# VectorE's first tap product in the PSUM words that TensorE sums; 2816 rows held back; a new order

## The chip, the cores and the metric

One core of one Trainium2 chip runs the program. The metric is device time in microseconds (us). Engines are written as the profile has them: PE is TensorE's matmuls and PEld its weight loads, DVE is VectorE, ACT is ScalarE, POOL is GpSimd, SP is SyncE, which issues most DMAs.

## The reference

A windowed mix of 7 tokens with softmax weights per head, then a top-1 mixture of experts over its result.

```python
# attention: B=8, S=3584, D=192, H=8 heads, K=7 taps, group=24
w = softmax(weight_gen, axis=-1)                      # [B, S, 8, 7]
out = einsum('bshk,bskhg->bshg', w, x_unf)            # x_unf[s, k] = x[s - 6 + k], zeros before 0
# experts: N=28672 tokens, D=192, E=8, F=1024
e_idx = argmax(x @ w_gate, axis=1)
for e in range(E):
    h = maximum(x[mask] @ w1[e], 0.0)                 # mask: e_idx == e
    out[mask] = gate_w[mask, None] * eom[mask, e, None] * (h @ w2[e])
```

`gate_w` is the softmax probability of the chosen expert, `eom` the sigmoid of `x @ w_output_gate`.

## The kernel before

**Units.** The 28672 tokens are cut into 32 units of 896 (128 partitions by 7 tokens). For each unit the front end loads x and the weights (SyncE), makes the softmax (VectorE, ScalarE), forms seven tap products of 128x1344 (x shifted by a tap, times that tap's weight), adds them, splits the sum into fp16 high and low parts in one of three row buffers `rt` (`sum_steps`), computes gate logits, ranks the tokens within their experts (`rank`: VectorE's scan, then two small TensorE matmuls `ps<-p,upper` and `ps<-p,ones`), and GpSimd scatters the rows into `srtd` in DRAM, sorted by expert: seven indirect DMAs for each unit.

**Taps.** `TAPS` gives a unit's first taps to GpSimd (`gap` tiles in SBUF) and the rest to VectorE. For units 0 to 5 (`u < PE_U`) GpSimd makes 4 and VectorE 3 (`vap` tiles in SBUF), and TensorE adds all seven by fp32 matmuls with an identity (`cf`) into one of two places of 1536 words in PSUM (`sum_free`, at 0 and 2560): per tap three matmuls, of 512, 512 and 320 columns (`add_steps`). A place comes free when VectorE has split the sum. From unit 6 on VectorE adds alone, into an accumulator in PSUM (`acc_steps`); there GpSimd makes 5 or 4 taps, by `POOL` and `SHARES`.

**Weights.** During the first units the weights of the 8 experts are loaded, split into fp16 pairs and written to `wd` in DRAM (`weight_steps`, `split_steps`).

**Tiles.** After each unit, `plan_rounds` decides how many expert tiles of a size may be released: rows that have come so far, less the rows taken, less a number that is held back (`HOLD`, six times the tile's rows: 3072 for 512). A released tile belongs to an expert that has enough rows; a slot that finds none points at dummy rows. `tile_load` has SyncE load the tile's rows transposed (`xT`), and the expert's weights (`wa`, `wb`, or `late` near the end), and TensorE does five matmuls for each of 8 blocks of hidden columns (`ps<-xT,wa`), ScalarE and VectorE make `hh` and `hl` from them, and TensorE 24 matmuls for each 128 rows (`ps<-wb,hh` and `ps<-wb,hl`). GpSimd scatters the results. There are 5 tiles of 256 rows after unit 2, 7 of 384 after units 4 to 6, then 43 of 512, and 5 of 256 and 15 of 128 among the last.

**Order.** Nothing is scheduled on the chip: every engine runs its instructions in the order in which this code writes them. `Order` is a planner that keeps a clock for each engine, and at each step lets the chain of work go on that can start first; among equals the rank decides (`RANK_...`), and `FAVOUR` moves single chains. Its costs are the constants at the end of the file (`LAT_P`, `LANDED`, `LAT_R` from VectorE's scan to the ranking matmul, and so on). So a changed constant moves instructions on all engines.

**Stirring.** `stir` puts matmuls on zeros (`ps<-pad,ident`, 256 columns) into TensorE's queue where the planner sees a gap over `STIR[0]` us, half as long as the gap; into an open sum, or, with a start flag, into a free place.

Of the kernel before, what the change touches and what calls it, by code (L numbers as in the profile page):

```python
# [27 lines left out]
def plan_rounds(units, every, size):  # L28

    left, rounds = 0, {}  # L30
    for u in range(units):
        left += size
        last = u == units - 1
        if u not in every and not last:
            continue
        subs = []
        for T, keep in SIZES(u, last):
            n = max(0, -(-(left - keep - HOLD(T)) // T))
            while n > 0:
                k = min(n, 8)  # L40
                subs.append((T, k))
                left -= k * T
                n -= k
        if last:
            subs.append((128, (left + NE * TAILK) // 128))
        rounds[u] = subs
    return rounds
# [259 lines left out]
def kernel(ctx: ExitStack, tc: tile.TileContext, x, wg, wgate, wogate, w1, w2, cst, out):  # L307
# [194 lines left out]
    def stir(gap):  # L502

        words, new = state["open"], False
        free = [at for t, at in sum_free if t <= T_.t]
        if words is None and free:
            words, new = ps[:, free[0] : free[0] + 256], True
        if gap < STIR[0] or words is None:
            return
        for _ in range(int(STIR[1] * gap / 0.112)):  # L510
            nc.tensor.matmul(words[:, 0:256], lhsT=ident, rhs=pad[:, 0:128].bitcast(F16), start=new, stop=new, skip_group_check=True)
# [139 lines left out]
    def load_steps():  # L651
        for u in range(1, NU):
            od.named(f"load {u}")
            od.cur.rank = (RANK_X if u <= X_EARLY else RANK_A, -1)
            yield from take(w_free, SP)
            w_load(u)
            U[u]["wt"] = od.cur.t
            od.cur.t = od.now
            od.add(softmax_steps(u), (RANK_A, u, 0), V, U[u]["wt"])
            yield from take(x_free, SP)  # L660
            if u >= XN:
                yield SP, lambda: "zero" in U[u - XN + 1]
            x_load(u)
            U[u]["xt"] = od.cur.t
            od.cur.t = od.now
# [43 lines left out]
    def tap_steps(eng, tag):  # L709

        for u in range(NU):
# [9 lines left out]
            if u >= PE_U and tag == "va":  # L721
                yield from acc_steps(u, taps)
                continue
            pairs = PAIRS if u < PE_U and tag == "ga" else 0
# [18 lines left out]
            used(u, tag)  # L743

# [50 lines left out]
    def add_steps(u, t, tag, kind):  # L795

        d = U[u]
        yield T_, lambda: "sum" in d or ("begun" not in d and (u == 0 or "sum" in U[u - 1]))
        if "begun" not in d:
            d["begun"] = 0  # L800
            _, at = yield from take(sum_free, T_)
            d["sum"], d["sum_at"] = ps[:, at : at + 1536], at
        n, flat = d["begun"], t.rearrange("p a b -> p (a b)")
        d["begun"] += 1
        for lo in (0, 512, 1024):
            hi = min(lo + 512, NV * GD)
            T_.matmul(d["sum"][:, lo:hi], lhsT=cf[:, 0:128], rhs=flat[:, lo:hi], start=(n == 0), stop=(n == K - 1 - PAIRS), skip_group_check=True)
# [3 lines left out]
        if n == K - 1 - PAIRS and state["open"] is d["sum"]:  # L811
            state["open"] = None
        if n == K - 1 - PAIRS:
# [305 lines left out]
    def tile_steps():  # L1119

        while "all" not in state or queue:
# [14 lines left out]
            d["ready"] = od.cur.t  # L1136
# [250 lines left out]
HOLD = lambda T: 6 * T  # L1387
TAILK = 79
RANK_W = 4.5
LAT = 0.0756  # L1390
LAT_S = 0.2324
LAT_P = 0.3614
LAT_T = 1.8143
LOCK = True
ARRIVE = 1.9478
LANDED = 0.5447
LAT_R = 1.1028
SLACK = 0.0352
SCATTER = 0.987
SMALL = 0.0762  # L1400
EAGER = 0, 0.2, (2, 3, 4)
BACK = 1.0
TURNS = (1536,)
# [15 lines left out]
POOL = (5,5,4)  # L1419
SHARES = {18: 5, 11: 4, 28: 4, 20: 4}  # L1420
FAVOUR = {}
PE_U = 6
STIR = 0.8, 0.5
GIVE = 1
RANK_X = 2.5
X_EARLY = 3
RANK_GATE = 4.5
FIRST_G = ()
DEFER = 4
WBX = 3.3548  # L1430
# [4 lines left out]
EARLY = {2: ((256, 0),), 4: ((384, 0),), 5: ((384, 0),), 6: ((384, 0),)}  # L1435
# [20 lines left out]
```

## Time and profile before

| | us |
|---|---|
| median of 3 runs (lowest, highest) | 1220.73 (1212.9, 1223.78) |
| profiled execution: its own time | 1223.71 |
| profiled execution: span | 1222.0 |
| PE busy in the span | 1120.0 |
| DVE busy | 955.9 |
| POOL busy | 841.5 |
| ACT busy | 616.6 |
| mean granted TensorE clock | 0.978 |

The span runs from the first to the last instruction of one execution. Busy time of an engine leaves out the time in which it waits. A stretch of the span has to be looked at by itself, since the first 150 us are spent on the front end and the weights, the middle on both the front end and the tiles, and the last 200 us on tiles alone. [...]

### The profile page before, as it was taken

How to read it: one execution, taken by the hardware profiler on the slowest of the kernel's cores; microseconds unless marked ns; L12 is line 12 of the kernel's file. 1: busy time of each engine (PE TensorE's matmuls, PEld its weight loads, DVE VectorE, ACT ScalarE, POOL GpSimd, SP SyncE). 2: the span in 40 equal slices, each digit the busy share in tenths (PEclk: the TensorE clock that was granted, in tenths of full speed). 3: DMA queues.
4: the chain of work that ended last, by engine and by line, in shares of the span. 5: the costliest groups of instructions: out<-in, count | busy, mean ns of one | idle time of the engine just before them, and what ended most of it. 6: DMA issues, size and time to landing. Idle time of an engine off the chain costs nothing.

```text
span 1222.0 us, 27128 instructions
## 1 busy us (share of the span) xinstructions
PE 1120.0 (92%) x9693; PEld 812.1 (66%) x9693; DVE 955.9 (78%) x1874; ACT 616.6 (50%) x1300; POOL 841.5 (69%) x620
## 2 busy tenths in 40 slices
PE   8987686899979999999999998899999999999897
PEld 4544375677657666666666666676666666798697
DVE  7999696999999979998999989899998653333231
ACT  4986553455555545455555544455544434434342
POOL 6678783777898868887888877678888554322122
PEclk9999898999989999999999999899999999999999
DMA  8989699998697979799799969887979696599992
GB/s 280 285 276 299 194 287 268 215 270 235 172 264 176 260 225 232 164 250 233 192 244 249 253 163 246 235 212 197 236 193 195 192 270 196 165 292 244 321 292 84
DMA packets 294952, 282.77 MB, mean 231 GB/s; under 512 B 229222, under 2 KB 254423, under 8 KB 294816
## 3 DMA queue, kind: packets, MB, share of 16 engines
q1 hardware_dynamic: 272976, 236.54, 73.0%
q0 software_dynamic: 21696, 44.30, 12.5%
q8 instruction: 76, 1.25, 0.4%
q14 instruction: 60, 0.49, 0.1%
q10 hardware_dynamic: 144, 0.20, 0.1%
HBM read 174.77 MB, written 60.28 MB: 192 GB/s over the span
## 4 chain that ended last, share of the span: by engine, by line
PE 58%; DVE 17%; DMA 9%; issue 8%; POOL 5%; ACT 1%; SPq 1%; another core or an unknown queue 0%; POOLq 0%; DVEq 0%; ACTq 0%
PE ps L207 58%; DVE ps L207 9%; DVE hl L207 4%; DMA wa<-wd 4%; POOL srtd L207 3%; DMA srtd<-rt,posi 2%; POOL gap L207 1%; DVE vt L207 1%; SPq L175 1%; DMA gt<-rt 1%; DMA meta<-srtd 1%; DVE rt L207 1%; POOL out_dram L207 1%; DVE lz L207 1%; DMA w<-in_wg_dram 1%
## 5 line engine op out<-in xcount | busy, mean ns | idle before, releaser
L207 PE MATMUL ps<-xT,wa 128*128 128x512 f16 (+3 forms) x2440 | 491.1, 350 | 42.5 <-DMA wa<-wd 12.8
L207 PE MATMUL ps<-wb,hh 128*128 128x192 f16 x3648 | 473.5, 247 | 8.2 <-ACT ys L207 4.4
L207 PE MATMUL ps<-wb,hl 128*128 128x192 f16 x1824 | 450.1, 247 | 1.4 <-issue 1.4
L207 DVE SCALAR_TENSOR_TENSOR hl<-ps,hh 128x512 f16<-128x512 f32 (+1 forms) x470 | 305.2, 666 | 172.0 <-ACT hh L207 124.0
L207 POOL TENSOR_TENSOR gap<-x,w 128x1344 f32<-128x1344 f32 x145 | 379.4, 2624 | 43.2 <-issue 14.8
L207 POOL DMA_INDIRECT out_dram<-ys,meta x220 | 218.4, 993 | 243.2 <-ACT ys L207 176.1
L207 PEld LDWEIGHTS <-wa 128*128 128x128 f16 x2440 | 226.8, 99 | 229.0 <-issue 47.7
L207 PEld LDWEIGHTS <-hh 128*128 128x128 f16 x3648 | 332.5, 98 | 53.7 <-issue 15.9
L207 ACT ACTIVATE hh<-ps 128x512 f16<-128x512 f32 (+1 forms) x470 | 267.7, 582 | 177.6 <-PE ps L207 147.9
L207 POOL DMA_INDIRECT srtd<-rt,posi x224 | 230.2, 1028 | 85.2 <-issue 57.8
L207 ACT ACTIVATE ys<-ps,sc 128x192 f32<-128x192 f32 x228 | 95.8, 420 | 288.4 <-PE ps L207 180.1
L207 DVE TENSOR_TENSOR ps<-ps,gap 128x1344 f32<-128x1344 f32 x121 | 187.9, 1553 | 0.4
L207 PEld LDWEIGHTS <-hl 128*128 128x128 f16 x1824 | 179.3, 98 | 0.9 <-issue 0.6
L207 DVE SCALAR_TENSOR_TENSOR rt<-ps,sx,rt 128x448 f16<-128x448 f32 x64 | 57.6, 910 | 7.4 <-DMA srtd<-rt,posi 2.5
L207 PE MATMUL ps<-xT,late 128*128 128x128 f16 (+2 forms) x560 | 59.9, 263 | 3.7 <-DMA late<-wd 3.7
L207 PE MATMUL ps<-gap,cf 128*128 128x512 f32 x144 | 60.7, 559 | 0.0
L207 DVE TENSOR_TENSOR ps<-ps,vt 128x1344 f32<-128x1344 f32 x35 | 54.4, 1555 | 0.0
L207 DVE TENSOR_TENSOR vt<-x,ps 128x1344 f32<-128x1344 f32 x35 | 54.1, 1545 | 0.1
L207 PEld LDWEIGHTS <-late 128*128 128x128 f16 x560 | 40.2, 98 | 16.5 <-DMA late<-wd 3.9
L207 ACT ACTIVATE rt<-ps 128x1344 bf16<-128x1344 f32 x32 | 41.3, 1291 | 17.2 <-DVE ps L207 9.5
L207 ACT ACTIVATE rt<-ps,sx 128x1344 f16<-128x1344 f32 x32 | 44.2, 1380 | 11.4 <-DVE sx L207 8.2
L207 PE MATMUL ps<-gm,gt 128*128 128x32 f16 x672 | 28.1, 177 | 20.1 <-ACT gt L207 10.4
(121 smaller groups left out, 809.2 us busy)
## 6 DMA issues: line engine op xcount, KB each, us to landing
wb<-wd SPq DMA_DIRECT2D x75, 768.5 KB
wa<-wd SPq DMA_DIRECT2D x61, 768.0 KB
x<-in_x_dram SPq DMA_DIRECT2D x32, 672.0 KB
late<-wd SPq DMA_DIRECT2D x14, 768.0 KB
wa<-wd SPq DMA_DIRECT2D x61, 128.0 KB
w<-in_wg_dram SPq DMA_DIRECT2D x32, 196.0 KB
wd<-wpb SPq DMA_DIRECT2D x8, 768.5 KB
st<-in_w_dram SPq DMA_DIRECT2D x8, 768.0 KB
```

The costliest lines, as they stand in the source:

```text
L175: r = f(*args, **kwargs)
L207: r = f(*args, **kwargs)
```

## The change

For units 0 to 5 VectorE's first tap product goes straight into the unit's words in PSUM (`base_steps`), and TensorE adds the other six onto it, none with a start flag. Ahead of everything twelve matmuls on zeros write both places once. A unit's additions on TensorE can begin when its first product is there. Stirring begins at a gap of 0.37 us, and never has a start flag. `HOLDS` holds back 2816 rows for 512-row tiles, not 3072; units 8 to 14 then release 2, 2, 1, 2, 2, 2 and 1 tiles, where they released 1, 2, 2, 2, 1, 2 and 2, and so on. 148 taps are GpSimd's, where 145 were. The other constants change the order alone. The tiles are as many of each size as before.

```diff
@@ -35,7 +35,7 @@
             continue
         subs = []
         for T, keep in SIZES(u, last):
-            n = max(0, -(-(left - keep - HOLD(T)) // T))
+            n = max(0, -(-(left - keep - HOLDS[T]) // T))
             while n > 0:
                 k = min(n, 8)
                 subs.append((T, k))
@@ -501,14 +501,18 @@
 
     def stir(gap):
 
-        words, new = state["open"], False
+        words = state["open"]
         free = [at for t, at in sum_free if t <= T_.t]
         if words is None and free:
-            words, new = ps[:, free[0] : free[0] + 256], True
+            words = ps[:, free[0] : free[0] + 256]
         if gap < STIR[0] or words is None:
             return
         for _ in range(int(STIR[1] * gap / 0.112)):
-            nc.tensor.matmul(words[:, 0:256], lhsT=ident, rhs=pad[:, 0:128].bitcast(F16), start=new, stop=new, skip_group_check=True)
+            nc.tensor.matmul(words[:, 0:256], lhsT=ident, rhs=pad[:, 0:128].bitcast(F16), start=False, stop=False, skip_group_check=True)
+
+    for _, at in sum_free:
+        for lo in range(at, at + 1536, 256):
+            nc.tensor.matmul(ps[:, lo : lo + 256], lhsT=ident, rhs=pad[:, 0:128].bitcast(F16), start=lo % 512 == 0, stop=False, skip_group_check=True)
 
     def scattered(ins, u):
 
@@ -656,7 +660,7 @@
             w_load(u)
             U[u]["wt"] = od.cur.t
             od.cur.t = od.now
-            od.add(softmax_steps(u), (RANK_A, u, 0), V, U[u]["wt"])
+            od.add(softmax_steps(u), (RANK_A, u, 0), V, U[u]["wt"] + (W_LATE if u > PE_U else 0.0))
             yield from take(x_free, SP)
             if u >= XN:
                 yield SP, lambda: "zero" in U[u - XN + 1]
@@ -720,6 +724,10 @@
                 tap_free["ga"].extend(f for f in tap_free[tag] if f[1] == tag)
             if u >= PE_U and tag == "va":
                 yield from acc_steps(u, taps)
+                continue
+            if tag == "va":
+                yield from base_steps(u, taps)
+                used(u, tag)
                 continue
             pairs = PAIRS if u < PE_U and tag == "ga" else 0
             while taps:
@@ -741,6 +749,28 @@
                 else:
                     d["gp"].append((t, kind, od.cur.t))
             used(u, tag)
+
+    def base_steps(u, taps):
+
+        d = U[u]
+        left = list(taps)
+        room = lambda: sum_free and (u == 0 or "sum" in U[u - 1])
+        while left:
+            yield V, lambda: "sum" in d or len(left) > 1 or room()
+            if "sum" not in d and room():
+                at, place = sum_free.pop(0)
+                od.cur.t = max(od.cur.t, at)
+                yield V
+                d["sum_at"] = place
+                full = ps[:, place : place + NV * GD]
+                product(V, full.rearrange("p (a b) -> p a b", b=GD), u, left.pop(0))
+                d["sum"], d["sum_t"], d["begun"] = ps[:, place : place + 1536], od.cur.t, 0
+                continue
+            _, kind = yield from take(tap_free["va"], V)
+            k = left.pop()
+            t = sum_tile(kind, f"vap{u}_{k}")
+            product(V, t, u, k)
+            od.add(add_steps(u, t, "va", kind), (RANK_A, u, 3), T_)
 
     def acc_steps(u, taps):
 
@@ -795,22 +825,20 @@
     def add_steps(u, t, tag, kind):
 
         d = U[u]
-        yield T_, lambda: "sum" in d or ("begun" not in d and (u == 0 or "sum" in U[u - 1]))
-        if "begun" not in d:
-            d["begun"] = 0
-            _, at = yield from take(sum_free, T_)
-            d["sum"], d["sum_at"] = ps[:, at : at + 1536], at
+        yield T_, lambda: "sum" in d
+        od.cur.t = max(od.cur.t, d["sum_t"])
+        yield T_
         n, flat = d["begun"], t.rearrange("p a b -> p (a b)")
         d["begun"] += 1
         for lo in (0, 512, 1024):
             hi = min(lo + 512, NV * GD)
-            T_.matmul(d["sum"][:, lo:hi], lhsT=cf[:, 0:128], rhs=flat[:, lo:hi], start=(n == 0), stop=(n == K - 1 - PAIRS), skip_group_check=True)
+            T_.matmul(d["sum"][:, lo:hi], lhsT=cf[:, 0:128], rhs=flat[:, lo:hi], start=False, stop=(n == K - 2 - PAIRS), skip_group_check=True)
         tap_free[tag].append((od.cur.t + LAT_P, kind))
         if n == 0:
             state["open"] = d["sum"]
-        if n == K - 1 - PAIRS and state["open"] is d["sum"]:
+        if n == K - 2 - PAIRS and state["open"] is d["sum"]:
             state["open"] = None
-        if n == K - 1 - PAIRS:
+        if n == K - 2 - PAIRS:
             d["total"] = d["sum"][:, 0 : NV * GD].rearrange("p (a b) -> p a b", b=GD)
             od.add(sum_steps(u), (RANK_B, u), S, T_.t + LAT_P)
 
@@ -1133,7 +1161,7 @@
                     row = SP.value_load(pads[0:1, e : e + 1], min_val=0, max_val=DUMMY - P)
                     scattered(SP.dma_start(out=srtd[bass.ds(row, P), :], in_=pad), u)
             d = tile_load(state["t"], T, ti, i, ([n for v, n in state["writers"] if v <= u], [n for v, n in state["writers"] if v > u]), ka, kb)
-            d["ready"] = od.cur.t
+            d["ready"] = od.cur.t + T_LATE
             state["t"] += 1
             ahead.append(d)
             od.cur.t = od.now
@@ -1384,22 +1412,24 @@
 
 
 RANK_H, RANK_Y, RANK_C, RANK_R, RANK_B, RANK_A, RANK_G = 1, 0, 2, 3, 4, 5, 6
-HOLD = lambda T: 6 * T
+HOLDS = {128: 768, 256: 1408, 384: 2304, 512: 2816}
 TAILK = 79
-RANK_W = 4.5
+RANK_W = 4.718
 LAT = 0.0756
 LAT_S = 0.2324
-LAT_P = 0.3614
-LAT_T = 1.8143
+LAT_P = 0.384
+LAT_T = 1.85
 LOCK = True
 ARRIVE = 1.9478
-LANDED = 0.5447
-LAT_R = 1.1028
-SLACK = 0.0352
+LANDED = 0.434
+LAT_R = 0.851
+SLACK = 0.038
 SCATTER = 0.987
-SMALL = 0.0762
+SMALL = 0.073
 EAGER = 0, 0.2, (2, 3, 4)
 BACK = 1.0
+W_LATE = 0
+T_LATE = 0.0
 TURNS = (1536,)
 LEAD = 3.3869
 STG = 4
@@ -1416,23 +1446,23 @@
 XB = 4
 MB = 8
 PRO_G = 4
-POOL = (5,5,4)
-SHARES = {18: 5, 11: 4, 28: 4, 20: 4}
-FAVOUR = {}
+POOL = (5, 5, 5, 4)
+SHARES = {11: 4, 28: 5, 20: 5, 2: 3, 4: 4, 29: 5, 6: 5, 23: 4, 1: 3, 24: 5, 27: 5, 9: 5, 0: 3}
+FAVOUR = {'evac 21 2': 0.4, 'exp 19': -0.1}
 PE_U = 6
-STIR = 0.8, 0.5
+STIR = (0.37, 0.49)
 GIVE = 1
-RANK_X = 2.5
+RANK_X = 2.124
 X_EARLY = 3
-RANK_GATE = 4.5
+RANK_GATE = 4.275
 FIRST_G = ()
 DEFER = 4
-WBX = 3.3548
+WBX = 3.58
 PAIRS = 0
 TURN_SP = True
 GT = 1
 TR_U = 5
-EARLY = {2: ((256, 0),), 4: ((384, 0),), 5: ((384, 0),), 6: ((384, 0),)}
+EARLY = {2: ((256, 0),), 4: ((384, 0),), 5: ((384, 0),), 6: ((384, 0),), 3: ((384, 0),)}
 EVERY = {*range(99)}
 MANUAL = ("SP", "DVE", "PE", "Activation", "Pool")
 
```

The rows below are the instructions as they stand on an engine, before and now.

TensorE at unit 0's additions, behind the opening stirring (`vap` is a tap of VectorE's, `gap` one of GpSimd's, `gss` belongs to the gate weights). Before:

```order
L511 MATMUL ps<-pad,ident 128x256
L207 MATMUL ps<-vap_4_180,cf 128x512 x2
L207 MATMUL ps<-vap_4_180,cf 128x320
L207 MATMUL ps<-gap_0_178,cf 128x512 x2
L207 MATMUL ps<-gap_0_178,cf 128x320
L207 MATMUL ps<-gss,ones_110 128x1
```

Now:

```order
L511 MATMUL ps<-pad,ident 128x256
L207 MATMUL ps<-gap_0_183,cf 128x512 x2
L207 MATMUL ps<-gap_0_183,cf 128x320
L207 MATMUL ps<-vap_6_195,cf 128x512 x2
L207 MATMUL ps<-vap_6_195,cf 128x320
L207 MATMUL ps<-gss,ones_110 128x1
```

Tap 4 of unit 0 is no longer added here, and GpSimd's first tap comes first; 56 stirring matmuls stand ahead, where 42 stood.

VectorE at the same place (`x_88` is unit 0's x, `w_152` and `w_164` unit 1's weights). Before:

```order
L207 TENSOR_TENSOR vap_4_180<-x_88,ps 128x1344
L207 TENSOR_TENSOR w_152<-w_152,ps 128x392
L207 TENSOR_TENSOR vap_5_229<-x_88,ps 128x1344
L207 TENSOR_REDUCE ps<-w_152 128x56
L207 TENSOR_TENSOR vap_6_244<-x_88,ps 128x1344
```

Now:

```order
L207 TENSOR_TENSOR ps<-x_88,ps 128x1344
L207 TENSOR_TENSOR w_164<-w_164,ps 128x392
L207 TENSOR_TENSOR vap_6_195<-x_88,ps 128x1344
L207 TENSOR_REDUCE ps<-w_164 128x56
L207 TENSOR_TENSOR vap_5_254<-x_88,ps 128x1344
```

The first product writes PSUM at the same place in the queue; the other two have changed places.

GpSimd at the scatters of units 1 (`rt_102`) and 2 (`rt_104`), with tap products of units 4 and 5 between them. Before:

```order
L207 DMA srtd<-rt_102,posi_900 262144x194
L207 TENSOR_TENSOR gap_3_992<-x_488,w_416 128x1344
L207 DMA srtd<-rt_102,posi_900 262144x194 x4
L207 DMA srtd<-rt_104,posi_1046 262144x194
L207 DMA srtd<-rt_102,posi_900 262144x194
L207 DMA srtd<-rt_104,posi_1046 262144x194
L207 TENSOR_TENSOR gap_0_1150<-x_653,w_648 128x1344
L207 DMA srtd<-rt_104,posi_1046 262144x194
L207 TENSOR_TENSOR gap_1_1196<-x_653,w_648 128x1344
L207 DMA srtd<-rt_104,posi_1046 262144x194
```

Now:

```order
L207 TENSOR_TENSOR gap_0_1002<-x_528,w_525 128x1344
L207 DMA srtd<-rt_102,posi_882 262144x194
L207 TENSOR_TENSOR gap_1_1028<-x_528,w_525 128x1344
L207 DMA srtd<-rt_102,posi_882 262144x194
L207 TENSOR_TENSOR gap_2_1073<-x_528,w_525 128x1344
L207 DMA srtd<-rt_102,posi_882 262144x194 x3
L207 TENSOR_TENSOR gap_3_1178<-x_528,w_525 128x1344
L207 DMA srtd<-rt_104,posi_1165 262144x194 x7
```

The tap products of unit 5 have moved from between unit 2's scatters to between unit 1's, and no scatter of unit 2 stands ahead of one of unit 1.

## Rows read from the trace of the kernel before

**Rows 1.** Busy time of each engine by stage (us; instructions in brackets).
```profile
core 0: us, PE busy (x) PEld busy (x) DVE busy (x) ACT busy (x) POOL busy (x), PEclk, DMA share, GB/s
0.00:80.00 80.00, 73.47 (x305) 40.07 (x306) 67.94 (x125) 58.87 (x96) 53.14 (x38) 1.00 0.92 282
80.00:151.30 71.30, 51.37 (x280) 28.31 (x279) 59.13 (x117) 44.41 (x80) 57.82 (x32) 0.95 0.77 248
151.30:310.50 159.20, 137.75 (x1285) 109.69 (x1286) 141.42 (x306) 76.72 (x184) 112.73 (x81) 0.95 0.95 250
310.50:463.20 152.70, 139.22 (x1181) 96.53 (x1180) 140.20 (x260) 78.92 (x171) 127.44 (x91) 0.97 0.85 224
```

**Rows 2.** Groups of instructions: xcount | busy us, mean ns | idle before, releaser.
```profile
L207 POOL TENSOR_TENSOR gap<-x,w 128x1344 f32<-128x1344 f32 x145 | 379.4, 2624 | 43.2 <-issue 14.8 <-PE ps L207 13.7 <-DMA x<-in_x_dram 5.3
...
L207 DVE TENSOR_TENSOR ps<-x,ps 128x1344 f32<-128x1344 f32 x26 | 40.3, 1549 | 0.1
...
L207 DVE TENSOR_TENSOR vap<-x,ps 128x1344 f32<-128x1344 f32 x18 | 27.9, 1548 | 0.6 <-PE ps L207 0.4
...
L511 PE MATMUL ps<-pad,ident 128*128 128x256 f16 x110 | 15.4, 292 | 4.3 <-ACT ident L456 4.3
```

**Rows 3.** Timeline, TensorE: start us, us, instruction xcount [idle before <-releaser].
```profile
14.49 2.42 PE L207 MATMUL ps<-gap,cf 128*128 128x512 f32 x6
16.75 0.28 PE L207 MATMUL ps<-gss,ones 128*128 128x1 f32 x2
```

**Rows 4.** The chain that ended last: start us, us, what.
```profile
12.13 33.10 PE ps L207 x101
...
53.40 25.77 PE ps L207 x121
...
115.95 8.14 DMA srtd<-rt,posi
...
136.27 7.05 DMA srtd<-rt,posi
```

**Rows 5.** Timeline from 111 to 127 us: GpSimd, ScalarE, TensorE.
```profile
111.14 4.51 POOL L207 DMA_INDIRECT srtd<-rt,posi  x1 [1.98 <-ACT rt L207]
...
124.28 0.22 ACT L207 ACTIVATE rt<-tok 128x14 int32<-128x14 f32 x1 [5.62 <-DMA srtd<-rt,posi]
...
126.33 0.24 PE L207 MATMUL ps<-gm,gt 128*128 128x32 f16 x3 [4.76 <-ACT gt L207]
```

**Rows 6.** Timeline at the first tile: SyncE's load, TensorE's first matmuls.
```profile
143.66 0.42 SPq L175 DMA_DIRECT2D meta<-srtd  x1
...
151.32 2.31 PE L207 MATMUL ps<-xT,wa 128*128 128x256 f16 x10 [4.74 <-DMA wa<-wd]
```

**Rows 7.** Two 512-row tiles, load and first matmul; the stretch behind the first, by engine.
```profile
341.44 1.87 SPq L175 DMA_TRANSPOSE xT<-srtd  x1
...
348.89 1.46 PE L207 MATMUL ps<-xT,wa 128*128 128x512 f16 x3 [5.68 <-DMA wa<-wd]
...
413.70 1.46 SPq L175 DMA_TRANSPOSE xT<-srtd  x1
...
421.16 1.04 PE L207 MATMUL ps<-xT,wa 128*128 128x512 f16 x4
...
345.40:352.20 6.80, 3.31 (x8) 1.19 (x9) 6.66 (x18) 0.90 (x4) 6.30 (x4) 0.50 1.05 303
```

**Rows 8.** TensorE's waits for ranks: sum us, times, longest; one of them; clock behind it.
```profile
PE ps L207 <- DVE p L207: 7.3, 3, 3.5
...
739.74 0.18 PE L207 MATMUL ps<-p,upper 128*128 128x8 f16 x1 [2.94 <-DVE p L207]
...
741.40:744.80 3.40, 3.40 (x14) 1.88 (x13) 3.07 (x15) 3.12 (x8) 2.07 (x2) 0.51 1.11 229
```

**Rows 9.** The page: the chain's shares of the span by engine.
```profile
PE 58%; DVE 17%; DMA 9%; issue 8%; POOL 5%; ACT 1%; SPq 1%; another core or an unknown queue 0%; POOLq 0%; DVEq 0%; ACTq 0%
```

## The prediction

> **What bounds the kernel now.** I read the stages first: busy time per engine between the first matmuls of chosen tiles [rows 1]. The reader is to see three regimes. Up to 80 us TensorE is busy 73.47 us of 80 and the DMA engines 92%. From 80 to 151.3 us TensorE has 20 us to spare, VectorE is busy 59.13 us of 71.3 and DMA 77%. From 151.3 us, where the first expert tile begins [rows 6], TensorE is busy 137.75 of 159.2 us, then 139.22 of 152.7, with VectorE beside it at 140.20 of 152.7 and GpSimd at 127.44.
>
> Then the chain that ended last. Two pieces of it are TensorE alone, 33.10 us from 12.13 and 25.77 us from 53.40 [rows 4]: these are the tap additions of units 0 to 3 with transposes and logits between them. After them the chain goes over scatters: the landing after 115.95 (8.14 us) and the one after 136.27 (7.05 us) [rows 4]. That last one is the end of unit 2's scatters; SyncE then issues the first tile's loads (143.66) and TensorE starts it at 151.32 after 4.74 us of waiting for its weights [rows 6]. Over the whole span the chain is 58% TensorE and 17% VectorE [rows 9]. So time is won by an earlier first tile, or by fewer TensorE waits behind it. The expert matmuls themselves are as many before and after, tile for tile.
>
> **The change, part by part.** The sum is made against the profiled execution's own 1223.7 us (span 1222.0 and 1.7 around it); the median of the runs, 1220.7, is 3.0 below that, and the result is moved by these 3.0.
>
> *Six additions fewer.* Each of units 0 to 5 loses one of seven additions. One costs 2.26 us of TensorE's queue: an addition started at 14.49, and the row behind it at 16.75 [rows 3]. Six make 13.6 us. Units 0 to 3 are added up while TensorE is the chain, so four count there: 9.0 us. Ahead of the first addition stand 56 stirring matmuls, not 42; 14 more at 0.14 us (15.4 us for 110 [rows 2]) are 2.0, but the 42 ended before the first tap was there, so I charge 0.6. That makes TensorE 8.4 us earlier at 80 us.
>
> Does the first tile get that? In the stretch from 80 us VectorE and the DMA queue have room for 12.2 us (71.3 less 59.13) and 16 us (23% of 71.3) [rows 1], so 8.4 is possible, and not much over 12. There is also a stall there that the new order leaves out. GpSimd's row at 111.14 is unit 2's first scatter, standing ahead of unit 1's last; it took 4.51 us and waited 1.98 for ScalarE; unit 1's last went out at 115.95 and landed 8.14 later; ScalarE, which needs unit 1's row buffer for unit 4, had idled 5.62 us at 124.28, and TensorE 4.76 us at 126.33 [rows 4, 5]. In the new order unit 1's seven scatters all stand ahead of unit 2's, and unit 2's seven in one run. Against it: unit 2's ranking now comes after unit 3's split, one more weight split and unit 5's softmax on VectorE. I take 8.5 us for the first tile in all. Bounds: nothing (stall gone, VectorE behind instead), and 13.6.
>
> *The product into PSUM.* Eighteen products of a tap stand before and after; six now write PSUM. A product that writes SBUF took 1548 ns, one that writes PSUM 1549 (26 of them, the accumulator of later units) [rows 2]. I take 0. [...] The two rows show 1 ns, and they decide. Behind the product in VectorE's queue stand the weight splits; it waits for its place in PSUM, which VectorE itself frees by the split of the unit two before it, so it waits for nothing but the stirring that TensorE may still be doing there.
>
> *More stirring.* 142 matmuls of this kind and 12 opening ones, not 110: 44 more, 6.2 us at 0.14. All stand ahead of the first tile. Where they fill a wait they cost nothing; behind 80 us TensorE has 20 us of waits [rows 1] to cover them. If all lay on the path, 6.2 us. I take 0.
>
> *2816 rows held back.* Half of the units from 8 to 30 release a 512-row tile one unit earlier (unit 8 two and not one, unit 12 two and not one). [...] But a tile of unit 11 is released by the same unit in both plans and was as tight: issued 413.70, started 421.16 [rows 7]. TensorE runs on to that one and waits there, unless unit 11 comes earlier too. So the idle 5.68 us come back, and I take only the slow clock, half of 6.8: 3.4 us. Bounds 0 and 9.1.
>
> *Three taps more on GpSimd* (148, not 145). Each spares VectorE one product, 1.55 us [rows 2], 4.7 in all, and costs GpSimd 2.62 each [rows 2], 7.9 over 800 us of which it idles some 17% (127.44 of 152.7 busy [rows 1]): hidden. If that cover were gone it would be 7.9. VectorE is on the chain for 17% of the span [rows 9]; 17% of 4.7 is 0.8 us, and I take 1.2, since its share must be higher in the stretch where it is loaded and the three taps lie. Bounds 0 and 4.7.
>
> *The other constants* only move instructions; what that makes is a rival below, and 0 here.
>
> Sum: 8.5 + 0 + 0 + 3.4 + 1.2 = 13.1 us. 1223.7 - 13.1 = 1210.6 for an execution like the profiled one, and with the 3.0 us 1207.6 for the median.
>
> **The rivals.**
>
> *Given back.* The first tile comes earlier and nothing is left of it at the end. For it: from 151.3 to 310.5 the DMA queues are at 95% [rows 1], so tiles of 256 and 384 rows may be limited by their weights' transfer and not by when they began. Against it: the same bytes are moved, and 77% before 151.3 leaves room to move some of them earlier. Only the 1.2 us and part of the clock stay: 1217 to 1221.
>
> *Slower: TensorE meets ranks that aren't there.* The planner now reckons with 0.851 us, not 1.1028, from VectorE's scan to the ranking matmul, so that matmul can stand earlier in TensorE's queue, and all expert matmuls queue behind it. At 739.74 that wait was 2.94 us, and from 741.4 to 744.8 the granted clock was 0.51; three such waits made 7.3 us in all [rows 8]. With 3.4 us at half clock behind each, one costs some 2.4 + 1.7 = 4.1 us. Three more take back all of the 13.1; six more make it 12 slower, 1233. Against it: 0.25 us earlier at 26 units is 6.5 us even if every one waits all of it, and the other engines' delays are reckoned longer now, not shorter.
>
> *More.* The same tuning takes waits away. From 151.3 to 463.2 TensorE idles 35 us [rows 1] and runs at 0.95 to 0.97 of its clock; if the whole bound of each term came (13.6, 9.1, 4.7) it would be 27.4 us, 1193. [...]
>
> *It doesn't do what it says.* A slot for 512 rows that finds no expert with 512 rows runs on dummy rows, and the rows left at the end go through the closing loop, 128 at a time. The first tile took from 143.66 to past 151.32 only to load [rows 6], so some 20 us a pass, 1240 and more. Counting the reference's experts unit by unit against both plans, no slot stays empty and nothing is left for the loop. So this needs other inputs.
>
> **How the numbers follow.** Forecast 0.48 (1199 to 1213), more 0.15 (about 1193), given back 0.25 (about 1219), slower 0.10 (1233), empty slots 0.02. The likeliest case's time is 1207.6. A change under 1% (1208.5 to 1232.9) is about what a measurement of this kernel can't tell from none. Of the forecast I count 0.7 as beyond 1% and 0.3 as within: faster 0.34 + 0.15 = 0.49, same 0.14 + 0.25 = 0.39, slower 0.12. From 1192 to 1224 holds all but the slower cases (0.12) and about a third of the case of more (0.06).
>
> **What the changed profile would show.** Right: 36 tap additions on TensorE, not 42; TensorE's first busy piece ends some 8 us sooner; no long GpSimd row between the scatters of units 1 and 2; the first tile's matmul at 143 +- 4 us, not 151.3; no wait of over 5 us near 345; the same last tiles behind it. Wrong: the first tile at 150 or later (VectorE, not TensorE, set it); the first tile early but the 512-row tile that began at 310.5 not (the DMA queues gave it back); many waits of the ranking matmuls for VectorE, with the clock at half behind them.

## The result, and the profile after

The changed kernel took 1206.59 us (median of 9 runs, 1204.59 to 1214.57) beside 1220.35 us for the kernel before: a ratio of 0.9901 between the means of the runs, 95% interval 0.9872 to 0.9930. The forecast was 1207.6. The total came out within about 1 us, but not where the sum had put it.

The busy time by stage, cut at the same four tiles as [rows 1] (start and end, length, busy us and instructions of PE, PEld, DVE, ACT, POOL; granted clock as a share of full speed, DMA share, GB/s):

```profile
0.00:80.00 80.00, 71.74 (x332) 41.61 (x333) 69.66 (x125) 58.89 (x96) 52.58 (x38) 0.98 0.89 278
80.00:153.30 73.30, 48.52 (x243) 26.54 (x241) 61.12 (x118) 44.25 (x80) 54.74 (x32) 0.86 0.76 250
153.30:314.90 161.60, 137.60 (x1291) 110.22 (x1292) 141.10 (x306) 79.97 (x188) 115.88 (x82) 0.94 0.95 250
314.90:454.50 139.60, 134.97 (x1178) 95.56 (x1178) 132.54 (x247) 73.80 (x161) 120.29 (x87) 1.00 0.91 232
```

The first tile starts at 153.3, which is 2.0 us later than before, and the first 512-row tile (tile 13) at 314.9, 4.4 us later. The stretch behind it is 139.6 us, not 152.7. The whole stretch from tile 13 to tile 54, in which both kernels run the same 41 tiles, first before, then after:

```profile
310.50:1062.00 751.50, 709.18 (x6060) 499.31 (x6059) 641.76 (x1264) 377.00 (x814) 580.67 (x434) 0.98 0.84 217
```
```profile
314.90:1049.60 734.70, 701.84 (x6059) 497.42 (x6059) 635.15 (x1261) 372.31 (x810) 585.15 (x435) 1.00 0.84 221
```

The matmuls are the same (6060 and 6059 records). TensorE idles 32.9 us in it, not 42.3 (length less busy), and its busy time falls by 7.3 us, at a granted clock of 1.00 and not 0.98. So the gain is +2.0 and +2.4 before tile 13, -16.8 from there to tile 54, -2.3 behind: -14.7, the difference of the spans (1222.0 and 1207.3).

The -16.8 are made at two places. Tiles 13 to 18 (up to the start of tile 19) take 103.9 us, not 110.7, and tiles 35 to 38 take 68.9, not 83.0; the tiles between take 3.2 us more and those behind 0.9. The larger place, before and after:

```profile
712.20:795.20 83.00, 73.52 (x614) 50.55 (x613) 71.39 (x134) 37.69 (x84) 57.77 (x45) 0.94 0.94 226
```
```profile
712.90:781.80 68.90, 68.15 (x594) 48.52 (x593) 66.29 (x139) 41.22 (x88) 59.91 (x44) 1.00 0.83 214
```

There TensorE idled 9.5 us before, 2.94 of them at the rank of [rows 8], with a granted clock of 0.94; now it idles 0.8 us at 1.00. No term of the forecast's sum is priced there.

The timeline at the tiles of [rows 6, 7] (start us, us, engine, instruction, xcount, idle before):

```profile
144.84 0.42 SPq L175 DMA_DIRECT2D meta<-srtd  x1
...
153.31 1.03 PE L207 MATMUL ps<-xT,wa 128*128 128x256 f16 x4 [5.74 <-DMA wa<-wd]
...
329.26 5.49 SPq L175 DMA_TRANSPOSE xT<-srtd  x1
...
348.83 1.03 PE L207 MATMUL ps<-xT,wa 128*128 128x512 f16 x4
...
405.28 1.49 SPq L175 DMA_TRANSPOSE xT<-srtd  x1
...
418.73 1.03 PE L207 MATMUL ps<-xT,wa 128*128 128x512 f16 x4
```

The load of the tile near 345 (tile 15) goes out 12.2 us sooner, that of unit 11's tile (tile 19) 8.4 us sooner, and TensorE waits at neither. The groups that answer to [rows 2, 9], first the tap work and the stirring, then the chain's shares:

```profile
L207 POOL TENSOR_TENSOR gap<-x,w 128x1344 f32<-128x1344 f32 x148 | 385.2, 2606 | 54.8 <-PE ps L207 21.1 <-issue 17.2 <-DVE w L207 5.1
L207 PE MATMUL ps<-gap,cf 128*128 128x512 f32 x144 | 61.5, 567 | 1.9 <-DVE ps L207 1.9
L207 DVE TENSOR_TENSOR ps<-x,ps 128x1344 f32<-128x1344 f32 x32 | 49.6, 1550 | 1.5 <-PE ps L511 1.1 <-DVE ps L207 0.2
L207 PE MATMUL ps<-vap,cf 128*128 128x512 f32 (+1 forms) x72 | 29.6, 547 | 1.2 <-DVE vap L207 1.2
L511 PE MATMUL ps<-pad,ident 128*128 128x256 f16 x130 | 20.5, 315 | 0.0
L207 DVE TENSOR_TENSOR vap<-x,ps 128x1344 f32<-128x1344 f32 x12 | 18.5, 1545 | 0.0
```
```profile
PE 60%; DVE 21%; issue 7%; DMA 5%; ACT 2%; POOL 2%; SPq 1%; another core or an unknown queue 1%; DVEq 0%; POOLq 0%; ACTq 0%
```

There are 144 + 72 = 216 matmul records of additions, six to an addition: 36 additions. The 32 products that now write PSUM take 1550 ns.

### The profile page after: what moved, and what is told of

Its sections match the earlier page's. It is cut to its first block, busy times and chain, and to the rows that moved or that the text cites. A ratio compares the mean times of both kernels' runs of the same rounds, so it can differ in the third digit from the quotient of the medians.

```text
span 1207.3 us, 27124 instructions
## 1 busy us (share of the span) xinstructions
PE 1107.7 (92%) x9689; PEld 810.5 (67%) x9689; DVE 952.7 (79%) x1873; ACT 615.0 (51%) x1300; POOL 845.5 (70%) x623
## 4 chain that ended last, share of the span: by engine, by line
PE 60%; DVE 21%; issue 7%; DMA 5%; ACT 2%; POOL 2%; SPq 1%; another core or an unknown queue 1%; DVEq 0%; POOLq 0%; ACTq 0%
PE ps L207 59%; DVE ps L207 11%; DVE hl L207 4%; DMA wa<-wd 2%; DMA srtd<-rt,posi 1%; DVE vt L207 1%; SPq L175 1%; DVE rt L207 1%; DVE wa L207 1%; PE ps L511 1%; POOL srtd L207 1%; ACT hh L207 1%; DMA out_dram<-ys,meta 1%; DVE lz L207 1%
## 5 line engine op out<-in xcount | busy, mean ns | idle before, releaser
L207 PE MATMUL ps<-xT,wa 128*128 128x512 f16 (+3 forms) x2480 | 505.1, 351 | 34.5 <-DVE hl L207 12.2
L207 POOL TENSOR_TENSOR gap<-x,w 128x1344 f32<-128x1344 f32 x148 | 385.2, 2606 | 54.8 <-PE ps L207 21.1
L207 PEld LDWEIGHTS <-wa 128*128 128x128 f16 x2480 | 231.0, 98 | 226.8 <-issue 35.7
L207 DVE TENSOR_TENSOR ps<-ps,gap 128x1344 f32<-128x1344 f32 x124 | 192.9, 1555 | 2.2 <-POOL gap L207 1.5
L207 DVE TENSOR_TENSOR ps<-x,ps 128x1344 f32<-128x1344 f32 x32 | 49.6, 1550 | 1.5 <-PE ps L511 1.1
L207 DVE TENSOR_TENSOR ps<-ps,vt 128x1344 f32<-128x1344 f32 x32 | 49.8, 1556 | 0.0
L207 DVE TENSOR_TENSOR vt<-x,ps 128x1344 f32<-128x1344 f32 x32 | 49.5, 1546 | 0.1
L207 ACT ACTIVATE rt<-ps 128x1344 bf16<-128x1344 f32 x32 | 41.3, 1290 | 14.1 <-DVE ps L207 8.3
L207 PEld LDWEIGHTS ps<-gap,cf 128*128 128x128 f32 x144 | 26.9, 198 | 27.1 <-issue 26.3
L207 PEld LDWEIGHTS <-gt 128*128 128x128 f16 x672 | 25.3, 97 | 27.1 <-ACT gt L207 12.8
```

The lines of the kernel that those rows point to most:

```text
L207: r = f(*args, **kwargs)
```

## The experiments

The change has four parts: **P**, the product into PSUM with six additions; **H**, 2816 rows held back; **S**, the new shares of GpSimd; **N**, the planner's other numbers (with two favoured instructions, except in e8). The theory of the prediction was that P carries most of the gain, through an earlier first tile. Its rivals were that H does, that S or N does, and that each set of parts is an order of its own. The table gives each run's ratio to the kernel before on the same chip, and of its one profiled execution when tiles 1 and 13 began and how TensorE's time went from tile 13 to tile 54. The ratios say how much; the profiled executions, which can lie some us beside their own median, say where. The three groups e1 to e4, e5 to e8 and e9 to e12 ran on three chips, on which the kernel before has medians of 1220.2, 1214.3 and 1216.3 us; its one profile is of an execution of 1223.7 us.

| kernel | parts | ratio, 95% interval | tile 1 | tile 13 | tile 13 to 54 | of it idle |
|---|---|---|---|---|---|---|
| before | - | 1 | 151.3 | 310.5 | 751.5 | 42.3 |
| after | PHSN | 0.9901, 0.9872 to 0.9930 | 153.3 | 314.9 | 734.7 | 32.9 |
| e1 | P SN | 0.9906, 0.9870 to 0.9941 | 153.6 | 314.3 | 735.4 | 32.8 |
| e2 | H | 1.0009, 0.9982 to 1.0036 | 152.3 | 309.8 | 748.9 | 43.4 |
| e3 | HSN | 0.9886, 0.9828 to 0.9945 | 147.8 | 309.3 | 740.4 | 37.7 |
| e4 | P | 1.0046, 1.0019 to 1.0073 | 145.9 | 299.6 | 769.1 | 51.0 |
| e5 | PH N | 0.9985, 0.9949 to 1.0022 | 150.6 | 308.9 | 746.6 | 39.2 |
| e6 | S | 1.0000, 0.9957 to 1.0044 | 151.0 | 313.4 | 742.1 | 36.6 |
| e7 | PHS | 0.9867, 0.9808 to 0.9925 | 147.6 | 302.4 | 738.0 | 34.3 |
| e8 | N | 1.0032, 1.0003 to 1.0060 | 149.0 | 310.2 | 755.0 | 46.2 |
| e9 | P S | 1.0046, 1.0018 to 1.0075 | 146.5 | 299.0 | 765.7 | 53.8 |
| e10 | HS | 0.9985, 0.9964 to 1.0005 | 151.5 | 310.0 | 740.9 | 36.8 |
| e11 | PH | 0.9886, 0.9853 to 0.9918 | 145.5 | 298.6 | 740.9 | 36.3 |
| e12 | additions out | 1.0047, 1.0017 to 1.0077 | 152.6 | 310.3 | 751.3 | 43.1 |

How far one execution can be trusted, the table itself tells. Up to the first tile e2, e6 and e10 run the instructions of before in the same order on each engine, and start that tile at 152.3, 151.0 and 151.5: about 1 us means nothing there. e6 and e10 have a ratio of 1.00, yet their stretch from tile 13 to tile 54 is some 10 us shorter than that of the one profile of before. And the stall at tiles 35 to 38 belongs to the order of before: e12, which keeps that order, takes 86.1 us there, while every other kernel of the table takes 69 to 74, those with a ratio of 1 or more too, which lose their time elsewhere. So that place by itself doesn't tell which part gains.

**e1, the hold undone in the changed kernel.**

```diff
-HOLDS = {128: 768, 256: 1408, 384: 2304, 512: 2816}
+HOLDS = {128: 768, 256: 1536, 384: 2304, 512: 3072}
```

> The changed kernel with its hold put back to 1536 and 3072 rows, all else as changed (the order is planned anew). Theory of the prediction (six additions fewer are the gain, made before the first tile): the hold is worth about 3.4 us, so 1210 us, and the tile near 345 us starts after a wait of some 5 us. Theory of the earlier release (the gain lies between 310 and 800 us, because tiles are released before TensorE runs dry): 1217 to 1221, the slow-clock stretches of 23.8 us between 222 and 976 us come back, first tile unchanged at 153. Theory of the order as a whole (no single part carries it): anything from 1207 to 1225, with the loss spread over stages.

The ratio is that of the change, so in this company the hold is worth nothing that the intervals would show. The timeline says why: the tile near 345 is loaded late again, but TensorE comes to it only at 348.45 and does not wait.

```profile
339.75 1.48 SPq L175 DMA_TRANSPOSE xT<-srtd  x1
...
348.45 1.03 PE L207 MATMUL ps<-xT,wa 128*128 128x512 f16 x4
```

**e2, the hold alone.**

```diff
-HOLD = lambda T: 6 * T
+HOLDS = {128: 768, 256: 1408, 384: 2304, 512: 2816}
```

> The kernel before with the hold of 1408 and 2816 rows alone. Theory of the prediction: 1217 us (3.4 us off 1220). Theory of the earlier release: 1206 to 1211, the wait of 5.68 us near 345 gone, and the 512-row tile of unit 11 earlier too. Theory of the order as a whole: 1215 to 1225.

No difference. The wait near 345 goes, and comes back at unit 11's tile with the same length and the same 6.8 us at a granted clock of 0.50 (the last row is the stretch behind it by engine):

```profile
345.37 0.81 PE L207 MATMUL ps<-xT,wa 128*128 128x512 f16 x3 [1.42 <-DVE hl L207]
...
416.35 1.50 SPq L175 DMA_TRANSPOSE xT<-srtd  x1
...
423.75 1.04 PE L207 MATMUL ps<-xT,wa 128*128 128x512 f16 x2 [5.60 <-DMA wa<-wd]
...
420.90:427.70 6.80, 3.95 (x10) 1.48 (x11) 6.73 (x11) 0.58 (x3) 6.16 (x5) 0.50 1.10 281
```

**e3, seven additions in the changed kernel.** The constants, hold and shares are as changed. The stirring is written as before, without the opening matmuls, and with the changed constants that makes 87 stirring matmuls, where the changed kernel has 142 with its opening ones; so this run undoes both.

```diff
 def add_steps(u, t, tag, kind):
-    yield T_, lambda: "sum" in d
+    yield T_, lambda: "sum" in d or ("begun" not in d and (u == 0 or "sum" in U[u - 1]))
...
-            if tag == "va":
-                yield from base_steps(u, taps)
```

> The changed kernel with seven additions a unit again (first product in SBUF, no opening matmuls, stirring as it was written before), with all constants, hold and shares of the changed kernel. Theory of the prediction: 8 to 9 us later at the first tile, so 162 us, and 1215 us at the end. Theory of the earlier release: first tile within 2 us of 153 (VectorE and the scatters set it, not TensorE), and 1205 to 1209 at the end. Theory of the order as a whole: 1205 to 1225 with no stage that stands out.

With seven additions the kernel is as fast as with six, and the first tile is 5.5 us earlier than with six (147.8, not 153.3). In the changed kernel's own company the prediction's main term has the wrong sign, at least together with the stirring.

**e4, the product alone**, in the kernel before.

```diff
+            if tag == "va":
+                yield from base_steps(u, taps)
...
-            T_.matmul(..., start=(n == 0), stop=(n == K - 1 - PAIRS), skip_group_check=True)
+            T_.matmul(..., start=False, stop=(n == K - 2 - PAIRS), skip_group_check=True)
```

> The kernel before with the product into PSUM and six additions alone (with the 12 opening matmuls; constants, shares and hold of 3072 as before). Theory of the prediction: first tile at 143 us instead of 151.3 and 1212 at the end. Theory of the earlier release: first tile at 149 to 153, 1218 to 1222. Theory of the order as a whole: 1215 to 1225.

Here the first tile does come early (145.9), and tile 13 by 10.9 us. Then it is lost: at the tile near 345 TensorE has to wait for a load that goes out at nearly the time of before, since the hold of 3072 gives the tile free only when unit 9 is scattered. Unit 9's last scatter starts at 336.9, and at 336.8 before: the early first tile hasn't made the front end earlier there.

```profile
339.85 1.47 SPq L175 DMA_TRANSPOSE xT<-srtd  x1
...
347.06 1.52 PE L207 MATMUL ps<-xT,wa 128*128 128x512 f16 x4 [4.89 <-DMA wa<-wd]
```

Tile 15 begins 1.8 us earlier than before, tile 19 already 6.4 us later. From tile 13 to tile 54 the stretch takes 17.6 us more, half of it (8.7) idle, the rest busy time (718.06 us, not 709.18); the granted clock is 0.96 from 310 to 450 us and 0.95 from 450 to 600, and 0.98 in both before. The kernel is slower than before by 0.5%.

**e5 to e8, shares and numbers, each undone and each alone.**

```diff
-POOL = (5, 5, 5, 4)
-SHARES = {11: 4, 28: 5, 20: 5, 2: 3, 4: 4, 29: 5, ...}
+POOL = (5,5,4)
+SHARES = {18: 5, 11: 4, 28: 4, 20: 4}
```

> The changed kernel with GpSimd's taps as before (145 of the 256, at the old units). After the runs so far neither the hold nor the six additions carry the gain of 14 us, so the shares and the planner's numbers are left. Theory of the shares (VectorE's taps set the pace of the units, and three fewer at better places are the gain): 1215 to 1221. Theory of the planner's numbers (delays, weights of the ready list, early tiles, stirring): 1205 to 1209. Theory that every part is an order of its own and the set was picked together: 1210 to 1225, and the single parts do not add up. The prediction's own price for it: 1.2 us, so 1208.

> The kernel before with the new shares of GpSimd alone. Theory of the shares: 1206 to 1211. Theory of the planner's numbers: 1217 to 1221 (the prediction's price of 1.2 us included). Theory of orders picked together: 1215 to 1228.

```diff
-RANK_W = 4.718
-LAT_R = 0.851
-STIR = (0.37, 0.49)
...
+RANK_W = 4.5
+LAT_R = 1.1028
+STIR = 0.8, 0.5
```

> The changed kernel with the planner's numbers as before (delays, weights of the ready list, early tiles, stirring, no favoured instructions), but with the product into PSUM, the hold of 2816 and the new shares. Theory of the shares: 1206 to 1210. Theory of the planner's numbers: 1217 to 1224. Theory of orders picked together: 1212 to 1228.

> The kernel before with the planner's numbers of the change alone (no product into PSUM, hold of 3072, old shares, no favoured instructions). Theory of the shares: 1217 to 1222. Theory of the planner's numbers: 1205 to 1210. Theory of orders picked together: 1212 to 1228.

(There are 224 taps, 7 for each of 32 units, not 256.) Shares alone do nothing that shows, numbers alone cost 0.3%. The numbers undone (e7) keep the whole gain, with the first tile at 147.6 and tile 13 at 302.4: in these executions the numbers lose the early first tile and win 3.3 us of it back behind tile 13. The shares undone (e5) lose nearly the whole gain. So of the four parts the shares are the only one that the changed kernel can't do without (e1, e3, e5, e7). No part alone is faster, so the question became which pair is; the pair of shares and numbers was not run.

**e9 to e11, the pairs of P, H and S under the old numbers.** Each is made of the edits above.

> The kernel before with the product into PSUM and the new shares (hold of 3072, the planner's numbers as before). Each of the two alone gave nothing (ratios 1.0046 and 1.000). Theory that the first tile is early but that the old shares give it back (product alone: tile 13 began at 299.6 and not 310.5, and the stretch from there to tile 54 was 769 and not 751 us): both together keep it, tile 13 near 300, that stretch near 740, ratio 0.985 to 0.992. Theory that the hold is the partner: ratio 0.998 to 1.003. Theory that any set is an order of its own: no better guess than 0.987 to 1.005.

> The kernel before with the new shares and the hold of 2816 (seven additions, the planner's numbers as before). Theory that product and shares are partners: tile 13 at 309 to 314, the stretch behind it near 745, ratio 0.995 to 1.000. Theory that the hold is the partner of the shares: 0.985 to 0.991. Theory that any set is an order of its own: no better guess than 0.987 to 1.005.

> The kernel before with the product into PSUM and the hold of 2816, but the shares as before (the planner's numbers as before). It is the run of 1195.9 us less the new shares. Theory that product and shares are partners: tile 13 near 300, the stretch behind it 760 us or more, ratio 0.999 to 1.006. Theory that the hold is the product's partner (it releases rows earlier to a TensorE that is earlier): 0.985 to 0.991. Theory that any set is an order of its own: no better guess than 0.987 to 1.005.

With the old numbers the eight kernels are clear: without P and H together the ratio is 0.9985 to 1.0046, with both it is 0.9886 (e11) and 0.9867 (e7). I had expected product and shares to be the partners; it is product and hold. The tile near 345 in e9, with the last scatter of unit 9 and the stretch behind:

```profile
342.60 0.98 POOL L207 DMA_INDIRECT srtd<-rt,posi  x1 [0.30 <-issue]
...
349.81 1.48 SPq L175 DMA_TRANSPOSE xT<-srtd  x1
...
358.00 1.03 PE L207 MATMUL ps<-xT,wa 128*128 128x512 f16 x2 [11.36 <-DMA wa<-wd]
...
349.50:363.20 13.70, 5.20 (x13) 1.89 (x14) 10.50 (x13) 3.85 (x5) 12.78 (x9) 0.50 1.02 244
```

and in e11:

```profile
319.04 2.28 SPq L175 DMA_TRANSPOSE xT<-srtd  x1
...
331.70 1.03 PE L207 MATMUL ps<-xT,wa 128*128 128x512 f16 x4
```

In e9 TensorE began the tile ahead of it, tile 14, at 315.2 and not at 325.6; then it idles 11.36 us, with 13.7 us at a granted clock of 0.50. In e11 the same tile was loaded at 319.04, ahead of unit 9's last scatter (337.2), and TensorE goes on without a wait, 26 us ahead of e9. e2 fits this: there the next gate, the load of unit 11's tile, was no earlier (416.35), while in e11 unit 11's load goes out 10.6 us sooner than in the kernel before (403.1 against the 413.70 of [rows 7]), and TensorE waits 3.57 us for it, not 5.60.

**e12, six additions left out and nothing moved.**

```diff
-            r = f(*args, **kwargs)
+            r = None if getattr(self, "mute", False) else f(*args, **kwargs)
...
+        T_.mute = n == 1
         for lo in (0, 512, 1024):
...
             T_.matmul(...)
+        T_.mute = False
```

> The kernel before with the second addition of each of units 0 to 5 left out of the computation (18 matmuls; that tap is missing in the output), its product still made on VectorE or GpSimd, every other instruction on every engine in the order of before. It is the bare price of six additions. The prediction: four of them on the chain, 9 us, TensorE's first busy piece ends some 8 us sooner and the first tile begins at 143 and not 151. Theory that VectorE and the scatters set the first tile: 148 to 151.3. For the end: ratio 0.992 to 0.995 if it is carried, 0.998 to 1.000 if the old shares give it back.

TensorE has 216 records of additions, not 252 (18 instructions leave 36 records), and the first tile is not earlier but at 152.6. The timeline of TensorE, and two stretches by engine:

```profile
35.06 0.38 PE L207 MATMUL ps<-wss,ones 128*128 128x2 f32 x2 [3.07 <-ACT sqd L207]
35.31 4.20 PE L207 MATMUL ps<-vap,cf 128*128 128x512 f32 x6
39.34 2.42 PE L207 MATMUL ps<-gap,cf 128*128 128x512 f32 x6
...
52.15 0.24 PE L207 MATMUL ps<-gm,gt 128*128 128x32 f16 x3 [2.16 <-ACT gt L207]
52.24 0.33 PE L207 MATMUL ps<-ident,rt 128*128 128x128 f16 x3
52.40 4.17 PE L207 MATMUL ps<-vap,cf 128*128 128x512 f32 x6
...
35.00:38.00 3.00, 2.94 (x6) 1.43 (x7) 2.86 (x4) 3.00 (x8) 0.15 (x1) 0.60 1.08 336
52.00:56.00 4.00, 3.85 (x11) 1.84 (x12) 2.79 (x3) 4.00 (x7) 0.00 (x0) 0.58 1.01 346
```

In the kernel before the same instructions stand at the same time with no wait between them:

```profile
35.24 0.28 PE L207 MATMUL ps<-wss,ones 128*128 128x2 f32 x2
35.38 2.50 PE L207 MATMUL ps<-vap,cf 128*128 128x512 f32 x6
```

The additions left out so far have become a wait of 3.07 us for ScalarE, and behind the wait the granted clock is 0.60 over 35 to 38 us and the next addition takes 4.20 us, not 2.50. The chain was TensorE only by a hair: ScalarE's squares and copies, for which it waits now, were due at nearly the time at which TensorE had been busy until then. The same comes a second time before 58 us (2.16 us of waiting, then 0.58 over 52 to 56 us and an addition of 4.17 us), and by unit 2's rank the kernel is 2.4 us late (109.0 against 106.6). Where the 0.5% at the end comes from, its profiled execution doesn't show: at tiles 13 and 54 it is within 0.4 us of that of before.

## Why the prediction was right, and where it was wrong

**Right by its total, and that is luck.** 13.1 us were forecast against 13.8 measured between the medians (1220.35 less 1206.59; by the ratio it is 12.1). The largest term, 8.5 us at the first tile, came out as a loss of 2.0 in the profiled executions, and 14.1 us that no term counts came at tiles 35 to 38. Which part of the change brings the gain in the changed kernel is not shown; product and hold are shown to be a pair under the old numbers alone.

**Six additions fewer, 8.5 us at the first tile: failed.** The step that failed is "units 0 to 3 are added up while TensorE is the chain, so four count there". The chain of waits names one engine at each moment; it does not say how far behind the next one is. e12 shows that it was hardly behind: the six additions by themselves bring the first tile nothing (152.6, where the order of before gives 151.0 to 152.3). In the changed kernel nothing of the 8.4 us that I had for TensorE at 80 us has reached unit 1's rank, which is 1.1 us later. Its row before and after:

```profile
83.10 0.17 PE L207 MATMUL ps<-p,upper 128*128 128x8 f16 x1
```
```profile
84.18 0.17 PE L207 MATMUL ps<-p,upper 128*128 128x8 f16 x1
```

In e4 it is at 82.88. Only behind that, and only where the planner may also move the work, under the old numbers (e4, e7, e9, e11), is something won: the first tile is 3.7 to 5.8 us earlier. The changed kernel has not even that. It ranks unit 2 late; the row of that rank, before and after:

```profile
106.61 0.17 PE L207 MATMUL ps<-p,upper 128*128 128x8 f16 x1 [1.99 <-DVE ps L207]
```
```profile
118.71 0.17 PE L207 MATMUL ps<-p,upper 128*128 128x8 f16 x1
```

I had named what stands against me there (the split and the softmax ahead of unit 2's ranking) and then given it no price. VectorE after, on the way to that rank:

```profile
107.80 0.39 DVE L207 TENSOR_REDUCE lz<-ps 128x112 f32<-128x224 f32 x1 [2.30 <-PE ps L207]
...
110.10 4.30 DVE L207 SCALAR_TENSOR_TENSOR wpb<-st,wsc,wpb 128x1536 f16<-128x1536 f32 x1
...
114.44 1.27 DVE L207 SCALAR_TENSOR_TENSOR wa<-st,wsc,wa 128x1024 f16<-128x1024 f32 x1
...
117.24 0.26 DVE L207 TENSOR_TENSOR_SCAN p<-segs,ps 128x56 f16<-128x56 f16 x1
```

Of the 9.4 us from the logits to the scan, 5.6 are the two splits shown. But the late rank alone doesn't place the first tile: unit 2's seven scatters then go out in one run, and the last of them leaves at 135.87, 0.4 us before that of [rows 4]. It only lands later. The last scatter and its landing in the chain, after, then in e3, where taps still stand between unit 2's scatters:

```profile
135.87 8.63 DMA srtd<-rt,posi
```
```profile
136.39 3.37 DMA srtd<-rt,posi
```

[rows 4] has 7.05. So I priced when the scatters are issued and not when the last one lands; that a run of scatters lands late fits these rows, and e1 and e5 with the same run, but was not tested by itself. The condition that I wrote down for being wrong, a first tile at 150 or later, is what came. The new scatter order is there, with no row of 4.5 us between units 1 and 2, and is worth nothing at the first tile.

**2816 rows held back, 3.4 us: mechanism right, size wrong.** The measured ratio alone is 1.0009 (e2). The wait near 345 is gone, as said. That the idle time comes back at unit 11's tile is what e2 shows within a tenth (5.60 for 5.68), and the slow clock (0.50 over 6.8 us), which I had counted as won, comes back with it: the term is 0 alone. What failed is adding the terms. Beside the product, under the old numbers, the hold is worth 1.6% (e4 and e11, 1.0046 and 0.9886; e9, on e11's chip, has 1.0046 too), because the one makes TensorE early and the other has a tile ready for it. That sentence stood in the prediction ("unless unit 11 comes earlier too") and was not carried into the sum. Under the new numbers the hold is worth nothing (e1).

**Three taps on GpSimd, 1.2 us: too small to tell alone, and not explained in company.** Alone 1.0000 (0.9957 to 1.0044), an interval that holds both 0 and the upper bound. Under the old numbers, beside product and hold, e11 and e7 don't differ. But under the new numbers, e5 against the change, the shares decide over 0.8% (measured on different chips), some 10 us, twice the upper bound of 4.7. Up to unit 25 the new shares give GpSimd one tap more at most, so VectorE's spared products can't be it. What it is stays open. Shares and numbers without product and hold were not run, and since the changed kernel keeps its gain without the product (e3) and without the hold (e1), that pair may carry the gain by itself.

**The product into PSUM at nothing:** right, 1550 ns for 1549. **More stirring at nothing** was not tried by itself. TensorE's records of it are 142 in all, 130 and the 12 opening ones, so 32 more than before and not the 44 of the sum, which counted the 12 twice. In e12 two waits that nothing fills, of 3.07 and 2.16 us, are followed by a granted clock of 0.60 and 0.58; that stirring would spare this was not shown.

**The planner's numbers at nothing:** near nothing as a sum (1.0032 alone, and from 0.9867 to 0.9901 beside the other three, within the intervals), wrong as a picture. They lose 12.5 us before tile 13 (e7 and the change, 302.4 and 314.9) and win some back behind it. Whether the change is faster or slower than e7 the intervals don't tell, so no version is shown to beat it.

**The rivals.** *Given back* is what the product does under the hold of 3072 (e4, e9), and it even overshoots: in e4 TensorE is busy 8.9 us longer from tile 13 to tile 54, beside the 8.7 us that it idles more, and in e9 11.36 us of idling at one tile go with 13.7 us at a granted clock of 0.50. *Slower by ranks that aren't there* did not happen: TensorE's waits for ranks fell from the 7.3 us of [rows 8] to 4.7. *More* was nearest to how the gain came: by waits taken away, among them the one at 739.74 that *Slower* took as its price for a wait.

## What to carry to other kernels

Time taken off an engine is won only as far as the next engine is behind it: at each piece of the chain look up when the second input of the next instruction is ready, and take no more than that. Two edits of which one makes an engine early and the other makes its work ready early must be priced as a pair; under the old numbers each by itself measures as nothing or as a loss, and a test one part at a time would drop both. Where every part also changes the whole order, as here, taking single parts out of the finished kernel gives another answer: without the product, or without the hold, it was as fast, and without the new shares nearly all was lost. A starved place downstream (here one tile's load, some 30 us behind) is a gate: price every gain ahead of it against the time at which the gate opens.

## What the runs showed of the hardware

**In e12 the addition behind the removed ones became slower.** There 3.07 us of idling were followed by a granted clock of 0.60 over 35 to 38 us, and six matmul records took 4.20 us, not 2.50; in e9 11.36 us of idling went with 13.7 us at 0.50. In the prediction a slow clock stands behind waits that the kernel before has ([rows 7, 8]) and, in *Slower*, behind more waits for ranks; no term has it behind waits that six additions fewer may open.

**A weight split on VectorE took 4.38 us beside a GpSimd product, and 1.27 us without one.** After, on VectorE and on GpSimd:

```profile
90.33 4.38 DVE L207 SCALAR_TENSOR_TENSOR wa<-st,wsc,wa 128x1024 f16<-128x1024 f32 x1
...
91.05 2.57 POOL L207 TENSOR_TENSOR gap<-x,w 128x1344 f32<-128x1344 f32 x1
...
110.20 2.57 POOL L207 TENSOR_TENSOR gap<-x,w 128x1344 f32<-128x1344 f32 x1
```

The same split of 128x1024 took 1.27 us at 114.44, when no product ran, and 4.38 at 90.33; the wpb split of 4.30 at 110.10 lies beside the product at 110.20, and one of that size without a product took 1.80 at 77.69. Both long ones end within 0.2 us of the product's end plus their own short time (94.71 against 94.89, 114.40 against 114.57), as if held until the product was done; that is my reading of two cases, and no run shows what holds them. Both splits' rows begin before the product's, by 0.7 and 0.1 us, and the products took 2.57 us each, where the mean of all 148 is 2.61. Another pair went the other way, first VectorE, then GpSimd:

```profile
121.95 1.78 DVE L207 SCALAR_TENSOR_TENSOR wpb<-st,wsc,wpb 128x1536 f16<-128x1536 f32 x1
```
```profile
123.05 3.11 POOL L207 TENSOR_TENSOR gap<-x,w 128x1344 f32<-128x1344 f32 x1 [4.88 <-PE ps L207]
```

There the split kept its short time and the product took 3.11 us. So where these splits landed against GpSimd's products was worth up to 3.1 us (4.38 less 1.27), and a planner that prices a split at one duration can't see it.
